# Transposing gathered tokens by products of 64 array rows each, into two PSUM banks

## The chip, the core and the metric

One Trainium2 chip, one core of it. The metric is the time of one execution on the device, in microseconds (us), as the median of several runs. TensorE, VectorE, ScalarE and GpSimd run instruction streams of their own, which meet at semaphores; SyncE issues DMA transfers.

## What is computed

A block attention and behind it a layer of experts in which each token goes to one expert of sixteen. All is FP32.

```python
# q, k, v: 8 x 8 x 576 x 64; softmax within chunks of 64 tokens
attn = softmax(scale * q_c @ k_c.T);  x = (attn @ v_c) as 4608 x 512
g = argmax(x @ w_group)                    # one of 4 groups
e = argmax(x[g] @ w_expert[g])             # one of 4 experts in it
h = maximum(x @ w1[g, e], 0)               # 512 -> 1024
out = g_weight * e_weight * (h @ w2[g, e])  # 1024 -> 512
```

## The kernel before

The attention stage writes the tokens into a scratch array in DRAM, sorted by expert. Then a loop (line 926 on TensorE, and one like it on each other engine) runs over *units*. A unit is up to 256 tokens of one expert: two token tiles of 128 rows, or one, or the half of one. The kind of a unit, which a table holds, chooses the branch: `pairs` for two tiles, `one` for one tile, `few` for at most 64 tokens.

Matrix products are made in the FP32R type, each value as a high part and a low rest, so layer 1 is three sums (high by high, high by low, low by high). For layer 1 the tokens must have features on the partitions. The unit's rows are gathered from DRAM into `xgr` (128 tokens x 2 tiles x 514), and TensorE transposes them: `XT(u, kind)`, line 757, makes four products per tile, each with a 128x128 piece of `xgr` as the weights and the identity as the moving operand, into one PSUM bank per tile (`pxt[0]`, `pxt[1]`, line 704). In the branches for two tiles `XT(u + 1)` stands between layer 1 (`L1p`, line 849) and layer 2 (`L2`, line 866) of unit u; in `one` it stands between the two groups of transposes `T` of the hidden layer (line 773), in `few` between two of `Tq` (line 779). It transposes one tile or two, by the kind of the unit to come, and waits for the gathers on the semaphores Ga and Gb.

ScalarE copies the transposed tokens as the high part into `xth` (`xe`, line 998, by `XE`, line 974), and VectorE subtracts to get the low part `xtl` (line 1074). Each waits with XE: ScalarE on XT, VectorE on ScalarE's copies, for each tile on its own. After XE stands, on both, the preparation of the next weights (`prep1`, `prep2`: casts on ScalarE, subtractions on VectorE). GpSimd waits on XT before it saves two columns of `xgr` (`carry2`) and issues the next gathers. Layer 1 of unit u + 1 waits for ScalarE's copies, and its third sum for VectorE's.

The attention stage makes its products in tiles of 64x64 of the array (lines 301 and 337), with transposes of 128x128 in FP32 between them (lines 325 and 367). Line 587 transposes the first tokens in FP32R, before the loop.

Of the kernel before, what the change touches and what calls it, by code (L numbers as in the profile page):

```python
# [9 lines left out]
F32 = mybir.dt.float32  # L10
# [9 lines left out]
P = 128  # L20
# [93 lines left out]
def moe_kernel(tc, qk, v, wgs, w1, w2, cst, out):  # L114
# [3 lines left out]
    with ExitStack() as ctx:  # L118
# [584 lines left out]
        word = fpool.tile([1, 1], F32, name="word")  # L703
        pxt = [ps.tile([P, 4, P], F32, name="pxt%d" % j) for j in range(2)]
        ph = [lgk if j == NL0 - 1 else ps.tile([P, 512], F32, name="ph%d" % j) for j in range(4)]
# [28 lines left out]
        with tc.tile_critical():  # L734
            with nc.Block() as blk:

                @blk.tensor
                def _(pe):
                    def W(n, x):
                        pe.wait_ge(S[n], x)  # L740
# [16 lines left out]
                    def XT(u, kind):  # L757
                        def tr(j, inc):
                            for c in range(4):
                                m = pe.transpose(pxt[j][:, c, :].bitcast(F32R), xgr[:, j, c * P:(c + 1) * P], identr)  # L760
                            m.then_inc(S["XT"], inc)

                        with pe.If(kind > 1):
                            W("Ga", 16 * u)
                            tr(0, 1)
                            W("Gb", 16 * u)
                            tr(1, 1)
                        with pe.Else():
                            W("Ga", 16 * u)
                            W("Gb", 16 * u)  # L770
                            tr(0, 2)

# [201 lines left out]
                def XE(eng, W, sem, op, u, kn, oph=None):  # L974
                    with eng.If(kn > 1):
                        W("XT" if sem == "XEa" else "XEa", 2 * u + 1)
                        op(0).then_inc(S[sem], 1)
                        W("XT" if sem == "XEa" else "XEa", 2 * u + 2)
                        op(1).then_inc(S[sem], 1)
# [14 lines left out]
                def _(ac):  # L994
# [3 lines left out]
                    def xe(u, kn):  # L998
                        XE(ac, W, "XEa", lambda j: ac.copy(xth()[:, :, half[j]], pxt[j]), u, kn)

# [69 lines left out]
                def _(ve):  # L1070
                    def W(n, x):
                        ve.wait_ge(S[n], x)

                    def xe(u, kn):
                        XE(ve, W, "XEd", lambda j: ve.tensor_sub(xtl()[:, :, half[j]], pxt[j], xth()[:, :, half[j]].bitcast(F32)), u, kn,
                           lambda: ve.tensor_sub(xth()[:, :, 64:P], pxt[0][:, :, 0:64], xth()[:, :, 0:64].bitcast(F32)))
# [352 lines left out]
```

## Time and profile before

| | us |
|---|---|
| median of 3 runs | 625.95 (625.27 to 626.41) |
| the profiled execution, by its own time | 621.86 |
| its span, first to last instruction | 620.2 |
| TensorE products busy | 581.9 (94%) |
| TensorE weight loads busy | 503.1 (81%) |
| VectorE busy | 365.8 (59%) |
| ScalarE busy | 263.5 (42%) |
| GpSimd busy | 154.2 (25%) |

The page gives times in microseconds. PE is TensorE's products, PEld its weight loads, which overlap products; DVE is VectorE, ACT ScalarE, POOL GpSimd, SP SyncE. Starts of products are exact, their ends are modelled, and a product's stated duration holds the time through the array, so products that follow each other overlap in these rows. The expert loop runs from about 180 us to the end.

### The profile page before, as it was taken

What the parts mean: (1) busy time and instruction counts of PE and PEld (TensorE: products, weight loads), DVE (VectorE), ACT (ScalarE), POOL (GpSimd) and SP (SyncE); (2) the same over time, 40 slices, a digit from 0 to 9 for tenths busy, and PEclk for the clock granted to TensorE, in tenths of its full rate; (3) what the DMA queues carried; (4) which work ended last, traced back from release to release, by engine and by line L of the source; (5) the groups of instructions that cost most, each with busy time, mean ns of one, the idle gap of its engine ahead of it and who ended that gap; (6) DMA issues with size and microseconds to landing.
All of it is one profiled execution on the core that took longest, in us unless ns stands there. A gap on an engine that the chain in (4) does not pass through costs nothing.

```text
span 620.2 us, 16208 instructions
## 1 busy us (share of the span) xinstructions
PE 581.9 (94%) x5711; PEld 503.1 (81%) x5712; DVE 365.8 (59%) x688; ACT 263.5 (42%) x367; POOL 154.2 (25%) x279
## 2 busy tenths in 40 slices
PE   7898988968699999989999999999999999999995
PEld 4676766846688989878889899989989988898984
DVE  4677878886568472127597674725425578853311
ACT  3454555646236251115485362625115365552111
POOL 0003334574413111111333212222111121321120
PEclk9898999889899999989999999999999999999998
DMA  8999878464559792116298854552712686821110
GB/s 311 423 396 380 271 277 299 139 234 155 170 155 376 256 323 95 66 29 241 106 339 308 317 201 155 187 193 79 268 51 95 235 315 249 320 91 66 34 38 30
DMA packets 43103, 128.23 MB, mean 207 GB/s; under 512 B 4590, under 2 KB 4974, under 8 KB 41136
## 3 DMA queue, kind: packets, MB, share of 16 engines
q1 hardware_dynamic: 32192, 93.93, 42.7%
q0 software_dynamic: 10864, 33.64, 15.1%
q8 instruction: 33, 0.54, 0.3%
q14 instruction: 14, 0.11, 0.1%
HBM read 106.40 MB, written 21.93 MB: 207 GB/s over the span
## 4 chain that ended last, share of the span: by engine, by line
PE 85%; issue 5%; DVE 4%; DMA 3%; ACT 1%; POOL 1%; SPq 1%; DVEq 0%; ACTq 0%; POOLq 0%
PE py L875 29%; PE ph L860 20%; PE lgk L860 7%; PE ph L844 5%; PE o L337 3%; PE sc L301 3%; PE py L892 2%; PE pxt L760 2%; PE lgk L367 2%; PE tp L325 1%; DMA qk<-in_qk_dram 1%; PE lgk L325 1%; PE tp L367 1%; PE sc L387 1%; PE ph L806 1%
## 5 line engine op out<-in xcount | busy, mean ns | idle before, releaser
L860 PE MATMUL ph<-xt,w1h 128*128 128x256 f32 x672 | 100.3, 286 | 2.7 <-issue 2.7
L860 PEld LDWEIGHTS ph<-xt,w1h 128*128 128x128 f32 x672 | 90.7, 194 | 4.4 <-issue 3.3
L1016 ACT ACTIVATE hth<-ph 128x512 fp32r<-128x512 f32 x43 | 25.7, 598 | 157.4 <-PE ph L860 154.1
L1343 POOL DMA_INDIRECT out_dram<-xl,io__2835 x37 | 39.2, 1059 | 163.2 <-DVE xl L1079 147.1
L1089 DVE TENSOR_TENSOR w1l<-w1r,w1h 128x2048 fp32r<-128x2048 f32 x28 | 63.0, 2289 | 13.1 <-ACT w1h L1003 11.1
L1093 DVE TENSOR_TENSOR w2l<-w2r,w2h 128x1024 fp32r<-128x1024 f32 x60 | 69.4, 1219 | 2.2 <-ACT w2h L1007 2.2
L875 PE MATMUL py<-w2h,hth 128*128 128x512 f32 x264 | 67.6, 398 | 0.0
L875 PE MATMUL py<-w2l,hth 128*128 128x512 f32 x264 | 65.3, 389 | 0.0
L875 PE MATMUL py<-w2h,htl 128*128 128x512 f32 x264 | 65.2, 389 | 0.0
L1079 DVE TENSOR_SCALAR xl<-py,io__2835 128x512 f32<-128x512 f32 x33 | 24.7, 749 | 67.8 <-PE py L875 67.8
L1112 DVE SCALAR_TENSOR_TENSOR htl<-ph,hth 128x512 fp32r<-128x512 f32 x40 | 27.4, 688 | 61.2 <-ACT hth L1016 60.8
L875 PEld LDWEIGHTS py<-w2l,hth 128*128 128x128 f32 x264 | 49.6, 188 | 10.5
L875 PEld LDWEIGHTS py<-w2h,htl 128*128 128x128 f32 x264 | 49.6, 188 | 10.3
L875 PEld LDWEIGHTS py<-w2h,hth 128*128 128x128 f32 x264 | 47.6, 188 | 10.1 <-ACT hth L1064 0.9
L860 PE MATMUL ph<-xt,w1l 128*128 128x256 f32 x336 | 54.7, 285 | 0.5 <-DVE w1l L1089 0.5
L1003 ACT CAST w1h<-w1r 128x2048 fp32r<-128x2048 f32 x28 | 52.1, 1903 | 2.6 <-issue 1.9
L1007 ACT CAST w2h<-w2r 128x2048 fp32r<-128x2048 f32 x28 | 52.3, 1923 | 0.0
L860 PEld LDWEIGHTS ph<-xt,w1l 128*128 128x128 f32 x336 | 46.8, 193 | 0.7 <-DVE w1l L1089 0.7
L337 PEld LDWEIGHTS o<-va,pT 64*64 64x64 f32 x1120 | 22.5, 147 | 19.4 <-issue 7.3
L337 PE MATMUL o<-va,pT 64*64 64x65 f32 x1120 | 28.3, 239 | 10.1 <-DVE x L355 5.4
L301 PE MATMUL sc<-qk 64*64 64x64 f32 x1152 | 27.6, 233 | 7.4 <-issue 4.4
L301 PEld LDWEIGHTS sc<-qk 64*64 64x64 f32 x1152 | 22.0, 141 | 14.9 <-issue 6.0
(286 smaller groups left out, 949.4 us busy)
## 6 DMA issues: line engine op xcount, KB each, us to landing
w1r<-in_moe_w_dram SPq DMA_DIRECT2D x30, 1024.0 KB, 5.2
w2r<-in_moe_w_dram SPq DMA_DIRECT2D x30, 1024.0 KB, 7.1
qk<-in_qk_dram SPq DMA_DIRECT2D x15, 1024.0 KB, 10.3
xgr<-xs POOLq DMA_DIRECT2D x38, 257.0 KB, 4.6
va<-in_v_dram SPq DMA_DIRECT2D x24, 390.0 KB, 7.5
qk<-in_qk_dram SPq DMA_DIRECT2D x6, 512.0 KB, 6.9
w1r<-in_moe_w_dram POOLq DMA_DIRECT2D x2, 1024.0 KB, 9.7
w2r<-in_moe_w_dram POOLq DMA_DIRECT2D x2, 1024.0 KB, 7.6
```

The lines of the kernel that those rows point to most:

```text
L301: nc.tensor.matmul(sc[cols, x, hp * CH:hp * CH + CH], lhsT=T[rows, 0, hp, cols], rhs=T[rows, 1, hp, cols], start=True, stop=True)
L337: nc.tensor.matmul(o[cols, x, hp * W:hp * W + W], lhsT=pT[rows, hp, cols], rhs=v_at(2 * t + c)[rows, hp], start=True, stop=True)
L844: m = pe.matmul(ph[n], a_[:, c, 0:P], w_[:, c, n * 512:(n + 1) * 512], start=(i == 0), stop=(i == 11))
L860: m = pe.matmul(ph[f // 2][:, f % 2 * 256:f % 2 * 256 + 256], w_[:, c, f * P:(f + 1) * P], a_[:, c, :], start=(i == 0), stop=(i == 11))
L875: m = pe.matmul(py[j], a_[:, f, half[j]], w_(b, f), start=(i == 0), stop=(i == 23))
L1003: lambda b, s, j: ac.copy(wt[b][0][:, s], w1r[j]), K1)
L1007: lambda b, s, j: ac.copy(wt[b][2 + j], w2r[j]), K2)
L1016: ac.activation(hth()[:, 2 * b:2 * b + 2, :], ph[b].rearrange("p (f t) -> p f t", f=2), AF.Relu).then_inc(S["Ha"], 1)
L1089: lambda b, s, j: ve.tensor_sub(wt[b][1][:, s], w1r[j], wt[b][0][:, s].bitcast(F32)), K1, js)
L1093: m = ve.tensor_sub(wt[b][4 + 2 * j + i], w2r[j][:, 2 * i:2 * i + 2], wt[b][2 + j][:, 2 * i:2 * i + 2].bitcast(F32))
L1112: ve.scalar_tensor_tensor(out=htl()[:, 2 * b:2 * b + 2, :], in0=ph[b].rearrange("p (f t) -> p f t", f=2), scalar=0.0, in1=hth()[:, 2 * b:2 ...
L1343: gp.indirect_dma_start(out, bass.IndirectOffsetOnAxis(ap=io[:, j, 0:1].bitcast(I32), axis=0), yb[:, j, :], None, bounds_check=N - 1, oob_ ...
```

## The change

Each transpose of a 128x128 piece becomes two, one of rows 0 to 63 and one of rows 64 to 127 of the token tile, on the array's rows of the same numbers. The two write to different banks: `pxt2` holds two banks, the first for the low rows of both token tiles, the second for the high rows. TensorE waits for both gathers first, and signals once, after the last product. ScalarE's and VectorE's accesses collect the two halves of a tile from the two banks, and each engine waits once, for all of what comes before it.

```diff
-        pxt = [ps.tile([P, 4, P], F32, name="pxt%d" % j) for j in range(2)]
+        pxt2 = ps.tile([P, 2, 4, P], F32, name="pxt")
+        pxt = [pxt2[:, j] for j in range(2)]
+        xhalf = lambda j: pxt2[:, :, :, 64 * j:64 * j + 64]
+        xrows = lambda z, j: z[:, :, half[j]].rearrange("p c (r t) -> p r c t", r=2)
...
                     def XT(u, kind):
-                        def tr(j, inc):
-                            for c in range(4):
-                                m = pe.transpose(pxt[j][:, c, :].bitcast(F32R), xgr[:, j, c * P:(c + 1) * P], identr)
-                            m.then_inc(S["XT"], inc)
-
+                        def tr(js):
+                            for j in js:
+                                for c in range(4):
+                                    for r in (slice(0, 64), slice(64, P)):
+                                        m = pe.transpose(pxt2[:, r.start // 64, c, 64 * j:64 * j + 64].bitcast(F32R),
+                                                         xgr[r, j, c * P:(c + 1) * P], identr[r, r])
+                            m.then_inc(S["XT"], 2)
+
+                        W("Ga", 16 * u)
+                        W("Gb", 16 * u)
                         with pe.If(kind > 1):
-                            W("Ga", 16 * u)
-                            tr(0, 1)
-                            W("Gb", 16 * u)
-                            tr(1, 1)
+                            tr((0, 1))
                         with pe.Else():
-                            W("Ga", 16 * u)
-                            W("Gb", 16 * u)
-                            tr(0, 2)
+                            tr((0,))
...
                 def XE(eng, W, sem, op, u, kn, oph=None):
                     with eng.If(kn > 1):
-                        W("XT" if sem == "XEa" else "XEa", 2 * u + 1)
+                        W("XT" if sem == "XEa" else "XEa", 2 * u + 2)
                         op(0).then_inc(S[sem], 1)
-                        W("XT" if sem == "XEa" else "XEa", 2 * u + 2)
                         op(1).then_inc(S[sem], 1)
...
-                        XE(ac, W, "XEa", lambda j: ac.copy(xth()[:, :, half[j]], pxt[j]), u, kn)
+                        XE(ac, W, "XEa", lambda j: ac.copy(xrows(xth(), j), xhalf(j)), u, kn)
...
-                        XE(ve, W, "XEd", lambda j: ve.tensor_sub(xtl()[:, :, half[j]], pxt[j], xth()[:, :, half[j]].bitcast(F32)), u, kn,
+                        XE(ve, W, "XEd", lambda j: ve.tensor_sub(xrows(xtl(), j), xhalf(j), xrows(xth(), j).bitcast(F32)), u, kn,
```

## Rows read from the trace of the kernel before

**Rows 1.** The page's first line: the profiled span.
```profile
span 620.2 us, 16208 instructions
```
**Rows 2.** The page's chain that ended last, by line.
```profile
PE py L875 29%; PE ph L860 20%; PE lgk L860 7%; PE ph L844 5%; PE o L337 3%; PE sc L301 3%; PE py L892 2%; PE pxt L760 2%; PE lgk L367 2%; PE tp L325 1%; DMA qk<-in_qk_dram 1%; PE lgk L325 1%; PE tp L367 1%; PE sc L387 1%; PE ph L806 1%
```
**Rows 3.** TensorE's waits, 180 to 620 us: total us, times, longest.
```profile
PE ph L860 <- issue: 2.7, 2, 1.8
PE ph L860 <- DVE w1l L1089: 0.5, 1, 0.5
...
```
**Rows 4.** Instructions of line 760: duration ns min/median/max, first and last start us.
```profile
L760 PEld LDWEIGHTS pxt<-identr,xgr x152: 138/140/145, 182.9 to 607.2; 128*128 128x128 f32 x152
L760 PE MATMUL pxt<-identr,xgr x152: 221/249/308, 183.1 to 607.2; 128*128 128x128 f32 x152
```
**Rows 5.** Timeline around eight transposes: start us, us, engine, line, what, count.
```profile
221.35 0.28 PE L860 MATMUL ph<-xt,w1h 128*128 128x256 f32 x1
...
221.47 0.80 PE L760 MATMUL pxt<-identr,xgr 128*128 128x128 f32 x8
221.67 0.60 ACT L1016 ACTIVATE hth<-ph 128x512 fp32r<-128x512 f32 x1 [1.07 <-PE ph L860]
...
222.10 0.71 PE L875 MATMUL py<-w2h,hth 128*128 128x512 f32 x2
```
**Rows 6.** Timeline around four transposes between the layers, 244.4 to 245.3 us.
```profile
244.16 0.65 PE L860 MATMUL ph<-xt,w1h 128*128 128x256 f32 x4
...
244.94 0.69 PE L875 MATMUL py<-w2h,hth 128*128 128x512 f32 x2
```
**Rows 7.** Timeline, TensorE, in a unit of one tile, around eight transposes.
```profile
261.70 0.27 PE L776 MATMUL lgk<-cs,xl 128*128 128x128 f32 x1
...
262.45 0.62 PE L776 MATMUL ph<-cs,xl 128*128 128x128 f32 x4
```
**Rows 8.** Timeline, TensorE, in a unit of one tile, around four transposes.
```profile
309.07 0.60 PE L776 MATMUL lgk<-cs,xl 128*128 128x128 f32 x4
...
309.98 0.66 PE L776 MATMUL ph<-cs,xl 128*128 128x128 f32 x4
```
**Rows 9.** Timeline, attention stage: from products of 128x128 to products of 64x64.
```profile
62.42 0.49 PE L367 MATMUL lgk<-cs,x 128*128 128x128 f32 x3
62.84 0.29 PE L301 MATMUL sc<-qk 64*64 64x64 f32 x4
```
**Rows 10.** Timeline, attention stage: 64x64 products and loads, and the 128x128 behind them.
```profile
49.24 0.22 PE L337 MATMUL o<-va,pT 64*64 64x65 f32 x2
...
48.76 0.56 PEld L337 LDWEIGHTS o<-va,pT 64*64 64x64 f32 x32
...
49.39 0.20 PEld L367 LDWEIGHTS tp<-cs,x 128*128 128x128 f32 x2
```
**Rows 11.** Timeline, 149.5 to 150.2 us: the first tokens' transposes, and a one-row product behind them.
```profile
149.55 0.40 PEld L587 LDWEIGHTS sc<-identr,xg0r 128*128 128x128 f32 x4 [0.97 <-ACT xT L368]
...
150.01 0.29 PEld L485 LDWEIGHTS sc<-cs,one 1*128 1x128 f32 x2
```
**Rows 12.** Timeline, TensorE: the first two layer-2 products behind products of 17 rows.
```profile
179.30 0.73 PE L892 MATMUL py<-w2l,hth 128*128 128x512 f32 x2
```
**Rows 13.** Timeline, 505 to 522 us: copies, first subtraction, and TensorE's wait.
```profile
516.38 1.06 ACT L999 CAST xt<-pxt 128x512 fp32r<-128x512 f32 x2
...
516.98 1.29 DVE L1075 TENSOR_TENSOR xt<-pxt,xt 128x512 fp32r<-128x512 f32 x2
...
520.52 0.50 PE L860 MATMUL ph<-xt,w1l 128*128 128x256 f32 x2 [0.54 <-DVE w1l L1089]
```
**Rows 14.** The whole chain in order of time (start, us, what); and the stretch 270:275 by engine, clock.
```profile
268.63 1.76 issue
270.39 7.50 PE ph L860 x48
...
270.00:275.00 5.00, 4.61 (x26) 4.62 (x27) 0.00 (x0) 0.00 (x0) 1.89 (x4) 0.66 0.09 30
```

## Prediction

> **What bounds the kernel now.** The first view is the head of the page and its chain of work: the profiled span is 620.2 us [rows 1], and TensorE carries most of it: the products of the expert layers lead, and the transposes of line 760, which the change rewrites, hold 2% of the chain [rows 2]. The second view is the list of what TensorE waited for from 180 us on, the expert loop: three kinds in 440 us, of 2.7, 0.5 and less [rows 3]. No gather of tokens and no copy out of PSUM is among them (waits too short for that list appear below), so the loop runs at TensorE's own pace: what its queue takes longer or shorter reaches the end one for one, except where something else is later. The third view is the instructions of line 760: 152 products, median 249 ns, and as many loads of 140 ns [rows 4]. Walking the loop's timeline finds them in 24 places: 14 with eight products (two token tiles), 10 with four.
>
> The fourth view is the timeline around one such place. After the last product of layer 1 at 221.35 come the eight transposes, first start 221.47, and the second layer at 222.10 [rows 5]. From the start of the last layer-1 product to the end of the second layer-2 product is 222.81 - 221.35 = 1.46 us. The eight starts spread over 0.80 - 0.25 = 0.55 us. So all transposes together hold some 12 us, and that is the stake: 2%.
>
> **What paces a transpose.** The same form of transpose runs after an idle stretch at line 587: its four weight loads take 0.40 us, so they start (0.40 - 0.14) / 3 = 0.086 us apart from the very first, while the load itself lasts 0.14 [rows 11]. In FP32, with the same 128 columns of weights, the second load starts 0.20 - 0.14 = 0.06 after the first [rows 10]. In every transpose the data are the weights (128 columns) and the identity moves. The change halves the rows and the moving columns, and leaves the 128 columns of each load; it makes two loads of one.
>
> **The change, part by part.** (1) Eight products become eight pairs, one of each pair on array rows 0 to 63, one on rows 64 to 127. That different tiles of the array load and multiply side by side the attention stage shows: 32 loads of 64x64 take 0.56 us, that is 8 rounds of four at about 0.06 [rows 10]. So I let the two of a pair overlap and ask for the round. No row shows a transposed load of 64 rows. Bounds: 0.06 a round, if only the load's stream counts and the rest of the 0.086 goes with the shorter product; 0.172, if the two loads of a pair follow each other at today's distance. I take 0.086, the row with the same operation, type and number of loaded columns. Then the body gains nothing: 7 x 0.086 = 0.60 against 0.55.
>
> The Trainium skill speaks for a gain here: its page TensorEngine Tiling, section Theoretical Speedup, gives up to 2x for a contraction of 64 rows or fewer. By it a round would be about 0.04 and the sum below 6.0 us lower. No row of this trace shows transposes of half height, so it stands among the rivals.
>
> (2) The array changes its tiling twice in each of the 24 places. The rows: from a 128x128 product to 64x64 ones the start moves from 62.42 + 0.49 - 0.27 = 62.64 to 62.84, 0.20 [rows 9]; a following product of the same tiling would start at the pace of layer 1, (0.65 - 0.28) / 3 = 0.12 [rows 6]. From 64x64 back to 128x128 it is 49.24 to 49.39, 0.15, and the first load is then no longer ahead of its product [rows 10]. A change of rows alone, with all 128 columns kept, pays too: line 485 loads one row after line 587, at 150.01, when the last transpose's load started at 149.55 + 0.40 - 0.14 = 149.81: 0.20 where the pace is 0.086 [rows 11]. The first layer-2 pair after a change of tiling takes 0.73 [rows 12] against 0.71 now [rows 5].
>
> The new walk for a place of eight between layers 1 and 2: 0.20 into the new tiling, 7 x 0.086 = 0.60, 0.06 until the last load has a product, 0.01 for its partner, 0.15 back, 0.73: 1.75 us against 1.46, so +0.29. Eight places are of this kind: 2.3 us. With four products the walk is 1.75 - 4 x 0.086 = 1.41; today it is from 244.16 + 0.65 - 0.28 = 244.53 to 245.63, 1.10 [rows 6]: +0.31 by these, +0.30 with the rounding, in seven places: 2.1 us.
>
> (3) In the units of one token tile the transposes stand between two groups of transposes of the hidden layer. Today from 261.70 to 262.45 + 0.62 = 263.07, 1.37 [rows 7]. New: 0.20 + 0.60 + 0.07 + 0.15 + 0.66 (four of them from a standing start [rows 8]) = 1.68: +0.31, six places: 1.9 us. With four products in such a unit today's stretch holds a wait: 309.07 + 0.60 - 0.27 = 309.40 to 310.64, 1.24 [rows 8], since the copy that the second group needs isn't done. New 1.68 - 0.34 = 1.34: +0.10, three places: 0.3 us. The first three parts are 2.3 + 2.1 + 1.9 + 0.3 = 6.6 us.
>
> (4) ScalarE's two copies now wait for the whole of XT, and VectorE's first subtraction for both copies. Between the layers this costs nothing: ScalarE is in the Relu from 221.67 to 222.27 [rows 5], past the last transpose's start (221.47 + 0.80 - 0.25 = 222.02), and layer 1 of the next unit, which needs the copies, comes after all of layer 2. One place has no such cover. At the end of the unit at 509 to 519 the copies run from 516.38 to 517.44 and the first subtraction starts at 516.98, between them; then VectorE makes w1l, for which TensorE waits 0.54 at 520.52 [rows 13]. Subtractions that start at 517.5 put all of that 0.5 later. Queued behind them on VectorE are w1l and w2l, and TensorE waits for the first; behind ScalarE's copies stand its casts of w2, which layer 2 needs much later. +0.5 us. Elsewhere the extra wait lies under layer 2.
>
> (5) Both gathers are now awaited ahead of all products. The list of TensorE's waits holds none for a gather [rows 3]; I cost this at nothing, hidden by the layer-2 and layer-1 work between their issue and their use. The strided access of the copies (two banks read at once) I cost at nothing too: both engines have the room, up to the place in (4). The gathers of the next unit follow the transposes on GpSimd's queue; these start 0.3 later, as does all that needs them.
>
> (6) XT stands seven times in TensorE's program, each with 12 more products and 12 more loads; see the third rival.
>
> **Sum.** 6.6 + 0.5 = 7.1 us. Against the profiled execution (621.86 us, of which the span is 620.2) that is 629.0; that execution lies 0.65% under the median of the runs shown, 625.95, to which I add it: **633.0 us**, 1.1% slower. What a measurement here can tell from no change is about 0.2%, 1.25 us.
>
> **Rivals.**
> First, the rounds are shorter. At 0.06 (0.059 unrounded) the sum loses 7 x 0.027 x 14 + 3 x 0.027 x 10 = 3.5: +3.6, 629.6 us. For it: the FP32 loads come at that distance [rows 10]. Against: the 0.086 was there when no earlier product was streaming [rows 11]. At half of today's body (0.55 / 14 = 0.04 a round) it loses 6.0: +1.1, 627.0; that asks for loads closer together than any row has them. This is the case that the rule of TensorEngine Tiling would give.
>
> Second, and on the other side: half the rows with all columns are no change of tiling, so nothing drains, and rounds are 0.06. Then the walk keeps its ends and the body goes from 0.55 to 0.41 in 14 places and from about 0.21 (244.94 - 244.53 [rows 6], less 0.12 ahead and 0.08 behind as in [rows 5]) to 0.18 in 10: -1.96 - 0.3 + 0.5 = -1.8, 624.2 us. It decides as soon as the drain costs less per place than the 0.14 that the body saves; today's rows say 0.2 to 0.3. Against it: line 485 after line 587 [rows 11].
>
> Third, fetching of code. At 268.63 TensorE stood for 1.76 us on "issue", that is, on nothing that another engine does, and the next 48 products took 7.50 [rows 14] where 48 x 0.12 = 5.76 is normal; the mean granted clock from 270 to 275 was 0.66, so part of that stretch ran at 1.2 GHz in place of 2.4, after the idle stretch. Together 3.5 us hang on where that code lies. More code ahead of it can move the stall away (629.5) or make a second one (636.5).
>
> Fourth, the loads of a pair don't overlap: rounds of 2 x 0.059 = 0.118 add 4.1 (637.2), of 0.172 add 11.0 (644).
>
> **How the numbers follow.** Forecast as summed 0.48; rounds of 0.06 0.15; halved rounds 0.06; no drain 0.06; stall gone 0.04, second stall 0.04; loads in turn at 0.118 0.12, at 0.172 0.05. The range runs from 626.5 to 638.0: it leaves out the no-drain case, the slowest, and a remainder of the halved one, about 0.15. Faster by over 0.2%: no drain and a little of the stall gone together with short rounds, 0.08. Within 0.2%: the halved rounds and such mixtures, 0.10. Slower: 0.82.
>
> **What will show it.** In the timeline of a place of eight: about 0.20 from the last layer-1 product to the first load of a transpose, loads in pairs with about 0.086 between pairs, and a visible gap of some 0.15 ahead of layer 2. The walk from the last layer-1 product to the end of the second layer-2 product should be 1.75; if it is under 1.46 the forecast is wrong in sign. At the unit like that of 509 to 519, VectorE's first subtraction should start after the second copy. The forecast is wrong if the gaps are missing, if pairs come faster than 0.07 or slower than 0.1, or if the total moves by more than the places add up to: then stalls on "issue" have moved.

## The result, and the profile after

The changed kernel takes 630.94 us (median of 20 runs, 621.86 to 635.67), the kernel before on the same chip 624.52 (20 runs, 618.76 to 630.49): 6.4 us or 1.0% more by these medians. The ratio on record, which is taken from fast runs alone since some executions of either kernel are slower as a whole, is 1.0133, 95% interval 1.009 to 1.0176: about 1.3% slower. The profiled execution of the changed kernel took 625.41 us by its own time. The head of its page, to hold against [rows 1]:

```profile
span 623.8 us, 16500 instructions
## 1 busy us (share of the span) xinstructions
PE 582.7 (93%) x5863; PEld 501.0 (80%) x5864; DVE 363.3 (58%) x688; ACT 264.0 (42%) x367; POOL 152.8 (24%) x279
```

TensorE issues 152 products more than before and is busy 0.8 us longer. The loss doesn't show in busy time; it must be in gaps. The two spans differ by 3.6 us only, since in this execution the attention stage, which the change doesn't touch, ended earlier: the first transposes start at 178.4 us, before at 183.1 [rows 4]. (In the profiles of this study that start lies between 178.4 and 192.9.) The fair measure is from the last product ahead of the first transposes to the end of TensorE's last product, "the loop" from here on: 430.85 us before, 439.24 after, +8.39. That is one execution of each kernel; the runs say 6.4 by the medians and 1.33% of 624.52 = 8.3 by the ratio.

The instructions of the rewritten line, against [rows 4]: duration in ns (min/median/max), first and last start.

```profile
L765 PEld LDWEIGHTS pxt<-identr,xgr x304: 133/136/139, 178.4 to 610.9; 64*128 64x128 f32 x152
L765 PE MATMUL pxt<-identr,xgr x304: 240/247/253, 178.4 to 610.9; 64*128 64x64 f32 x152
```

Half the rows in a load, and the load lasts as long as before: 136 ns against 140. A place of eight between the layers, the timeline to hold against [rows 5]:

```profile
215.73 0.64 PE L863 MATMUL ph<-xt,w1h 128*128 128x256 f32 x4
216.30 0.84 PE L765 MATMUL pxt<-identr,xgr 64*128 64x64 f32 x16
216.41 0.60 ACT L1018 ACTIVATE hth<-ph 128x512 fp32r<-128x512 f32 x1 [1.07 <-PE ph L863]
217.07 0.97 PE L878 MATMUL py<-w2h,hth 128*128 128x512 f32 x3
217.19 1.07 ACT L1001 CAST xt<-pxt 128x512 fp32r<-128x512 f32 x2 [0.17 <-PE pxt L765]
```

The last layer-1 product starts at 215.73 + 0.64 - 0.28 = 216.09. From there it takes 0.21 to the first transpose (before 0.12), the 16 starts spread over 0.84 - 0.25 = 0.59 (before 0.55), and from the last of them to layer 2 it is 217.07 - 216.89 = 0.18 (before 0.09). So the body is as long as it was, and both ends have a gap that wasn't there. Single records show the pairs: 0 to 17 ns from the first of a pair to the second, 84 ns (median) from pair to pair. The walk to the start of the second layer-2 product is 1.06 us before and 1.32 after; to that product's end, as the prediction has it, 1.46 before and 1.71 after, where 1.75 was forecast.

What TensorE waited for in the loop, against [rows 3]:

```profile
PE ph L863 <- issue: 3.9, 2, 2.5
PE ph L863 <- DVE w1l L1091: 1.1, 1, 1.1
PE pxt L765 <- DMA xgr<-xs: 0.9, 1, 0.9
PE lgk L787 <- DVE xl L1227: 0.3, 1, 0.3
```

Three rows differ: "issue" 3.9 in place of 2.7, w1l 1.1 in place of 0.5, and a gather that wasn't in the list at all. The gather's place in the timeline:

```profile
338.17 0.64 PE L863 MATMUL ph<-xt,w1h 128*128 128x256 f32 x4
...
339.72 0.85 PE L765 MATMUL pxt<-identr,xgr 64*128 64x64 f32 x16 [0.90 <-DMA xgr<-xs]
```

And in the chain, by time (start, us, what):

```profile
331.57 7.88 DMA xgr<-xs
339.45 0.26 issue
```

The last layer-1 product starts at 338.53, the second gather's last packet lands at 339.45: the start of the transposes is 1.18 behind that product in place of 0.21, 0.97 lost. The chain's 0.26 behind the landing is the way from it to the first product. The gather was not issued later than before: 6.96 us ahead of that layer-1 product, 6.97 before; it took longer to land. The unit that the prediction's step (4) speaks of:

```profile
518.25 1.05 ACT L1001 CAST xt<-pxt 128x512 fp32r<-128x512 f32 x2
519.34 1.29 DVE L1077 TENSOR_TENSOR xt<-pxt,xt 128x512 fp32r<-128x512 f32 x2 [0.47 <-ACT xt L1001]
522.88 0.51 PE L863 MATMUL ph<-xt,w1l 128*128 128x256 f32 x2 [1.12 <-DVE w1l L1091]
```

VectorE's first subtraction now starts behind both copies (518.25 + 1.05 = 519.30), and TensorE waits 1.12 for w1l where it waited 0.54 [rows 13].

Last the stalls on "issue": 2.54 at 230.80 and 1.35 at 269.76, before 0.96 and 1.76 [rows 3, 14]. The first of them in the timeline, and the stretch behind it (stretch, its length, busy us of PE, PEld, DVE, ACT, POOL, then the granted clock):

```profile
230.80 0.73 PE L863 MATMUL ph<-xt,w1h 128*128 128x256 f32 x4 [2.54 <-issue]
```

```profile
232.10:235.50 3.40, 3.40 (x19) 3.40 (x18) 0.00 (x0) 0.20 (x1) 0.31 (x2) 0.50 0.06 25
```

As at [rows 14], the granted clock fell behind a stall: to 0.50, 1.2 GHz, in the stretch shown, after some 1.3 us of products. The loss to the low clock is the same in both (the 96 products behind the stall start over 12.98 us in either kernel, over 11.39 at full clock: 1.6), so the net is 3.89 - 2.72 = 1.2 us.

The ledger of the loop, by walking all 24 places in both traces:

| | forecast, us | measured, us |
|---|---|---|
| 24 places, without the gather | 6.6 | 5.5 |
| gather at 339 us | 0 | 0.97 |
| w1l | 0.5 | 0.58 |
| stalls on "issue" and the clock behind them | 0 | 1.2 |
| rest | | 0.1 |
| sum | 7.1 | 8.4 |

### The profile page after: what moved, and what is told of

It reads as the page before. It is cut to its first block, busy times and chain, and to the rows that moved or that the text cites. A ratio compares the mean times of both kernels' runs of the same rounds, so it can differ in the third digit from the quotient of the medians.

```text
span 623.8 us, 16500 instructions
## 1 busy us (share of the span) xinstructions
PE 582.7 (93%) x5863; PEld 501.0 (80%) x5864; DVE 363.3 (58%) x688; ACT 264.0 (42%) x367; POOL 152.8 (24%) x279
## 4 chain that ended last, share of the span: by engine, by line
PE 78%; DVE 6%; issue 6%; DMA 5%; POOL 2%; ACT 1%; DVEq 0%; SPq 0%; POOLq 0%; ACTq 0%
PE py L878 28%; PE ph L863 18%; PE lgk L863 6%; PE ph L847 4%; PE o L337 3%; PE sc L301 3%; PE pxt L765 2%; PE py L895 2%; PE lgk L367 1%; DMA xgr<-xs 1%; PE ph L809 1%; DMA qk<-in_qk_dram 1%; PE tp L325 1%; PE py L832 1%; DMA xs<-x,pos 1%
## 5 line engine op out<-in xcount | busy, mean ns | idle before, releaser
L863 PE MATMUL lgk<-xt,w1h 128*128 128x256 f32 x224 | 33.7, 283 | 0.0
```

The costliest lines, as they stand in the source:

```text
L863: m = pe.matmul(ph[f // 2][:, f % 2 * 256:f % 2 * 256 + 256], w_[:, c, f * P:(f + 1) * P], a_[:, c, :], start=(i == 0), stop=(i == 11))
```

## The experiments

My theory: the pace of a transpose is that of loading 128 columns, which half the rows don't shorten; the two row tiles load side by side, so a pair takes what one full transpose took; and each change of tiling costs about 0.1 us at either end. The rivals: the pace is that of the queue or of the 64-column products, and the gaps at the ends are the waits that the change moves.

Each run below stands beside runs of the kernel before on the same chip; their median is in brackets. A time without a ratio is that of a single run, so there the trace is the evidence and not the time.

### What sets the pace: the order of the halves

```diff
-                            for j in js:
-                                for c in range(4):
-                                    for r in (slice(0, 64), slice(64, P)):
+                            for r in (slice(0, 64), slice(64, P)):
+                                for j in js:
+                                    for c in range(4):
```

> The changed kernel, with all low-row halves of XT first and then all high-row halves, so that neighbours in the queue lie on the same array rows. Theory (two row tiles load side by side, each tile takes a load every 0.085 us): the 16 starts of a place spread over 15 x 0.085 = 1.28 us in place of 0.595, the 8 starts of a smaller one over 0.60 in place of 0.257; 14 x 0.68 + 10 x 0.34 = 13 us more than the changed kernel. Rival (the 0.085 is the time of a pair, that is 0.04 a product, whatever the rows): spreads unchanged, no difference to the changed kernel.

640.86 us (628.28), ratio 1.0189, 1.0142 to 1.0236.

```profile
207.61 1.19 PE L765 MATMUL pxt<-identr,xgr 64*128 64x64 f32 x16
```

The starts spread over 1.19 - 0.25 = 0.94 in a place of eight and over 0.27 in a place of four. The theory wanted 1.28 (0.60 in a place of four), the rival 0.595: neither holds as stated. Single records show how it comes about: four starts alone, 83 to 86 ns apart, then four pairs (8 to 14 ns inside a pair, about 84 from pair to pair), then four alone again at 83 to 87. Each row tile takes a load each 0.085 us, as the theory says, and the two work side by side. But the halves of a pair needn't be neighbours in the queue: the second tile's loads begin when about four of the first tile's eight are still to start. The rows don't name the half, so which product is which is inferred from the counts and the order in the code. In a place of four, where the distance is only four, nearly all overlap. The theory's pace stands, its picture of the queue doesn't.

### What sets the pace: the kind of load

The changed kernel with ordinary products in place of transposes; and the kernel before with two ordinary full-height products per block, each with 64 moving columns.

```diff
-                                        m = pe.transpose(pxt2[:, r.start // 64, c, 64 * j:64 * j + 64].bitcast(F32R),
-                                                         xgr[r, j, c * P:(c + 1) * P], identr[r, r])
+                                        m = pe.matmul(pxt2[:, r.start // 64, c, 64 * j:64 * j + 64],
+                                                      xgr[r, j, c * P:(c + 1) * P], identr[r, r], start=True, stop=True)
```

> The changed kernel, with each half transposed by an ordinary FP32R product with the identity in place of the transpose operation; precision of the tokens is not kept. Rows, columns, banks and order are the same; the weight load is the ordinary one, which lasts 0.19 us at 128 columns against 0.14. Theory (the load sets the pace of a pair): pairs 0.11 us apart, spread of a place of eight blocks 7 x 0.112 + 0.01 = 0.80 us against 0.595, of four 0.35 against 0.257. Rival (the moving product sets it): 0.085 or less, spread 0.6. The ends of a place (0.21 ahead, 0.18 behind) stay by both.

```diff
-                                m = pe.transpose(pxt[j][:, c, :].bitcast(F32R), xgr[:, j, c * P:(c + 1) * P], identr)
+                                for r in (slice(0, 64), slice(64, P)):
+                                    m = pe.matmul(pxt[j][:, c, r], xgr[:, j, c * P:(c + 1) * P], identr[:, r], start=True, stop=True)
```

> The kernel before, with each 128x128 transpose made as two ordinary FP32R products of full height, with half of the identity's columns moving each; precision of the tokens is not kept. No change of tiling. Theory (the load of 128 columns sets the pace, the moving columns don't): 16 products 0.112 us apart, spread 15 x 0.112 = 1.68 us for eight blocks, 0.78 for four; lead 0.12 and end 0.09 as in the kernel before, no gap. Rival (halving the moving columns shortens the pace): 0.06 or less a product, spread 0.9 or less.

639.66 and 647.67 us (628.28 for both). The loads (duration in ns, min/median/max), of the halves and of the full height:

```profile
L765 PEld LDWEIGHTS pxt<-identr,xgr x304: 182/188/188, 189.7 to 625.0; 64*128 64x128 f32 x152
```

```profile
L761 PEld LDWEIGHTS pxt<-identr,xgr x304: 186/192/193, 187.7 to 633.2; 128*128 128x128 f32 x152
```

A place of eight in each, with the last layer-1 products ahead and layer 2 behind, first the halves, then the full height:

```profile
203.78 0.64 PE L863 MATMUL ph<-xt,w1h 128*128 128x256 f32 x4
204.34 1.08 PE L765 MATMUL pxt<-identr,xgr 64*128 64x64 f32 x16
205.35 1.19 PE L878 MATMUL py<-w2h,hth 128*128 128x512 f32 x4
```

```profile
202.63 0.64 PE L861 MATMUL ph<-xt,w1h 128*128 128x256 f32 x4
203.11 1.87 PE L761 MATMUL pxt<-identr,xgr 128*128 128x64 f32 x16
204.82 0.47 PE L876 MATMUL py<-w2h,hth 128*128 128x512 f32 x1
```

An ordinary load lasts 188 to 192 ns, a transposed one 136 to 140, with half the rows or all of them. The pairs of halves come 0.112 apart, but for a first interval of 0.13 (spread of eight 0.81, of four 0.36), and the full-height products 0.112 apart, but for a first one of 0.03 (1.59 and 0.70; 1.68 and 0.78 were expected). The product is the same 64 columns as in the changed kernel, where the pace is 0.085, and the data moved are the same: what changed is the operation, and with it the load's time, and the pace went with that. In the second of these kernels there is no gap at the ends (0.12 and 0.11), where the array keeps one tiling; in the first there is one at both (0.21 and 0.20; 0.21 and 0.18 were expected).

### What sets the pace: FP32, in halves and in full height

In FP32 the loads of a transpose come as close as 0.06 [rows 10]. First the changed kernel in FP32, then the kernel before.

```diff
-                                        m = pe.transpose(pxt2[:, r.start // 64, c, 64 * j:64 * j + 64].bitcast(F32R),
-                                                         xgr[r, j, c * P:(c + 1) * P], identr[r, r])
+                                        m = pe.transpose(pxt2[:, r.start // 64, c, 64 * j:64 * j + 64],
+                                                         xg[r, j, c * P:(c + 1) * P], ident[r, r])
```

> The changed kernel, with the halves transposed in FP32 in place of FP32R: same rows, columns, banks and waits. In the kernel before an FP32 transpose's second load started 0.06 us after the first, an FP32R one's 0.086 after. Theory (the load paces a pair, and its price goes by the type): pairs 0.06 apart, the spread of a place of eight 0.43 in place of 0.595, of four 0.19 in place of 0.257; the two changes of tiling stay, so a place of eight still takes 0.1 us more than before the change. 14 x 0.165 + 10 x 0.07 = 3.0 us under the changed kernel, 2.5 over the kernel before (5.5 less 3.0). Rival (FP32 streams its moving columns at half the rate, 0.109 for 128, and that paces it): 0.085 or more a pair.

```diff
-                                m = pe.transpose(pxt[j][:, c, :].bitcast(F32R), xgr[:, j, c * P:(c + 1) * P], identr)
+                                m = pe.transpose(pxt[j][:, c, :], xg[:, j, c * P:(c + 1) * P], ident)
```

> The kernel before with its transposes in FP32 in place of FP32R, in full height, so with no change of tiling: the partner of e7_fp32_halves, which had the halves in FP32. Theory (a transpose takes the longer of its load and its product; in FP32 the load takes up to 0.06 us and the product of 128 moving columns takes longer than that, as the hidden layer's FP32 transposes, which start 0.109 apart at 261.4 us in the kernel before, suggest): the starts of eight spread over 7 x 0.109 = 0.76 in place of 0.55, of four over 0.33 in place of 0.21; 14 x 0.21 + 10 x 0.12 = 4.1 us above the kernel before, 0.65%. Against the halves' 0.488 and 0.238 that would mean that half-height products do help, where the product and not the load sets the pace. Rival (the load sets the pace here too, at 0.06): spread 0.42 and 0.18, the ends as in the kernel before, 14 x 0.13 + 10 x 0.03 = 2.1 us below it, 0.35%.

637.11 us (628.8) for the halves; 631.01 (625.68) for the full height, ratio 1.007, 1.0034 to 1.0106. A place of eight in the timeline of each:

```profile
205.38 0.71 PE L765 MATMUL pxt<-cs,xgr 64*128 64x64 f32 x16
```

```profile
204.33 1.04 PE L760 MATMUL pxt<-cs,xgr 128*128 128x128 f32 x8
```

In halves the pairs come 0.060 to 0.065 apart, but for the first interval of 0.11, and the starts spread over 0.488 (of four over 0.238), where the theory wanted 0.43 and 0.19; in full height each transpose takes 0.109, and the spread is 0.763 (0.327), the theory's 0.76 and 0.33. So in full height the product sets the pace, and here the halves do what one would hope of them: 0.488 in place of 0.763. (Whether load or product sets the 0.06 of the halves, no run tells.) With both changes of tiling the walk of eight is 1.19 in halves and 1.23 in full height, a gain of 0.04; that of four 0.94 against 0.79, a loss. In FP32R, where the load sets the pace, there is nothing to gain and the two changes are still paid. That is the whole case. Against the kernel before, FP32 loses either way: its walks are 1.06 and 0.72. The loop of the halves in FP32 is 7.3 us longer than that of the kernel before, where 2.5 was expected: 3.3 in the places, 0.5 for a gather, 0.5 for w1l, and the rest stalls on "issue" and the low clock.

The Trainium skill, TensorEngine Tiling (Array Packing), section Theoretical Speedup, whose "up to 2x" the prediction held as a rival, is thus borne out in part, and only where the load isn't the limit: 0.763 / 0.488 = 1.6 for FP32, 0.55 / 0.59 = 0.9 for FP32R. The Trainium skill, TensorE: Matmul & The Clock Gate, section LDWEIGHTS (loading the stationary operand), says that a load's time goes with its columns and not with its rows; the 136 and 140 ns agree for the rows. No run here varied the columns of these loads; in the kernel before, ordinary loads of one row and 128 columns (line 485) last 184 ns, and loads of 17 rows and one column (line 915) 78.

### The price of a change of tiling

Half the blocks by half-height transposes, half by two full-height products; first all of one kind and then all of the other, then in turn. The copies and waits are those of the changed kernel. The two kernels differ in one line:

```diff
-                            for j, c in sorted(((j, c) for j in js for c in range(4)), key=lambda z: (z[1] % 2, z)):
+                            for j, c in sorted(((j, c) for j in js for c in range(4)), key=lambda z: z):
```

> The changed kernel, with half of the 128x128 blocks (odd c) made by two ordinary full-height products of 64 moving columns, all of them behind the halved transposes of the even blocks; precision of these tokens is not kept. Two changes of tiling in a place, as in the changed kernel, but one of them now inside the place. By the pieces measured so far (pairs 0.085, full-height products 0.112, 0.21 ahead, 0.18 at the change back, 0.112 behind) the walk from the last layer-1 product to the second layer-2 product's start is 1.9 us for eight blocks and 1.3 for four. It is the base for the next kernel.

> The same products as in the grouped kernel, with the blocks in turn: eight changes of tiling in a place of eight, four in one of four. Theory (each change drains the array and leaves the next load uncovered, 0.12 us over the normal pace): 6 x 0.12 = 0.7 us more than the grouped kernel in a place of eight, 0.23 in a place of four, 12 us in all. Rival (a change costs only against the long products of the layers, inside XT the short ones hide it): walks as in the grouped kernel, within 0.1 us.

648.4 us grouped, 658.66 in turn (628.8 for both). The start of a place of eight, in turn:

```profile
205.26 0.25 PE L768 MATMUL pxt<-identr,xgr 64*128 64x64 f32 x2
205.44 0.41 PE L766 MATMUL pxt<-identr,xgr 128*128 128x64 f32 x2
205.78 0.25 PE L768 MATMUL pxt<-identr,xgr 64*128 64x64 f32 x2
205.95 0.41 PE L766 MATMUL pxt<-identr,xgr 128*128 128x64 f32 x2
```

The same products, the same loads, six changes more: the walk is 1.88 grouped and 2.505 in turn, 0.63 / 6 = 0.105 per change; in a place of four 1.26 and 1.474, 0.21 / 2 = 0.105. The theory expected 0.7 and 0.23. A start behind a change comes 0.175 to 0.18 late into the full height (205.26 to 205.44) and 0.207 into the halves (from 205.44 + 0.41 - 0.28 = 205.57 to 205.78), each time about 0.1 more than the pace. Both kernels change the operation with the tiling, transposes for the halves and ordinary products for the full height. That the operation isn't what costs, the two runs with ordinary products alone show: 0.21 and 0.20 at the ends with halves, 0.12 and 0.11 in full height. So the gaps of the changed kernel, 0.21 and 0.18, are the price of its two changes of tiling and of no wait.

### The waits without the halves

The kernel before with the change's waits: both gathers first, one signal, ScalarE behind all of XT, VectorE behind both copies.

```diff
+                        W("Ga", 16 * u)
+                        W("Gb", 16 * u)
                         with pe.If(kind > 1):
-                            W("Ga", 16 * u)
-                            tr(0, 1)
-                            W("Gb", 16 * u)
-                            tr(1, 1)
+                            tr((0, 1))
...
-                        W("XT" if sem == "XEa" else "XEa", 2 * u + 1)
-                        op(0).then_inc(S[sem], 1)
                         W("XT" if sem == "XEa" else "XEa", 2 * u + 2)
+                        op(0).then_inc(S[sem], 1)
```

> The kernel before, with the waits of the change alone: both gathers first, one signal after all transposes, ScalarE's copies and VectorE's subtractions each after all of what comes before. Theory: spreads and ends of the 24 places as before (0.55, 0.21), TensorE's wait for w1l in the unit of 64 tokens near 511 to 521 us grows from 0.54 to about 1.1 us, nothing else moves; +0.5 us in all, too little to see in the time. Rival (the wait hides there as it does elsewhere): 0.54.

628.12 us (628.28). All places are those of the kernel before (spread 0.55 and 0.21, ends 0.12 and 0.08), but for two of TensorE's waits:

```profile
PE py L890 <- ACT hth L1013: 1.3, 1, 1.3
PE ph L858 <- DVE w1l L1086: 1.0, 1, 1.0
```

w1l costs 1.0 where it cost 0.54, so the prediction's step (4) comes from the waits alone. The other row lies ahead of the loop and is found in kernels with and without these waits (1.2 in the kernel with more code, below). At the tenth place, the one at 339 us of the changed kernel, the first transpose starts 0.26 behind the last layer-1 product in place of 0.12, and the spread is 0.63 in place of 0.55, 0.22 in all: TensorE waited for the second gather, which landed with the last layer-1 product (345.38 both). In the kernel before it landed 0.16 ahead of that product (339.83, the product at 339.99). From landing to first transpose it takes 0.26, so the cover that step (5) counted on was, by an estimate from these numbers, 0.02 us thick for transposes that start 0.12 behind the product, and 0.11 for those of the changed kernel, which start 0.21 behind it.

### The second gather, awaited late

The changed kernel, with the second gather awaited only ahead of the second tile.

```diff
-                            m.then_inc(S["XT"], 2)
+                            return m
 
                         W("Ga", 16 * u)
+                        with pe.If(kind > 1):
+                            tr((0,))
                         W("Gb", 16 * u)
                         with pe.If(kind > 1):
-                            tr((0, 1))
+                            tr((1,)).then_inc(S["XT"], 2)
                         with pe.Else():
-                            tr((0,))
+                            tr((0,)).then_inc(S["XT"], 2)
```

> The changed kernel, with the second gather awaited only ahead of the second token tile's transposes, as in the kernel before; the first tile's eight half transposes run as soon as the first gather is there. Theory (the wait of 0.97 us near 339 us comes from the second gather's late landing): the first tile's transposes, about 0.35 us with their change of tiling, move into the wait, which shrinks by about 0.35 us or vanishes where the gather lands earlier; every other place stays as in the changed kernel, 0.25 us above the kernel before, but for a few hundredths that the second branch may take; time within 0.2% of the changed kernel, 1.2% above the kernel before. Rival (the first gather, or something else, is what comes late): the first tile's transposes start no earlier than they did, and the wait stays whole.

632.51 us (627.03), ratio 1.0094, 1.0056 to 1.0132. TensorE's waits hold no gather:

```profile
PE ph L865 <- issue: 3.5, 2, 2.1
PE py L897 <- ACT hth L1020: 1.2, 1, 1.2
PE ph L865 <- DVE w1l L1093: 1.1, 1, 1.1
PE lgk L789 <- DVE xl L1229: 0.3, 1, 0.3
```

This tells nothing of the order of the waits: in this execution the second gather landed at 345.69, 0.6 ahead of the last layer-1 product (346.29), so there was nothing to shorten. The time from issue to landing of that transfer varies: 6.81 us before, 6.38 here, 5.72 to 6.82 in four further kernels in full height, 7.24 to 7.88 in the changed kernel and four others with its halves, 6.60 in one more of these. In the kernel before, the changed one and this one it is issued 3.9 us behind the first of the two loads of the next layer-2 weights, and the DMA engines are busy to over 9 tenths for most of its way. Why it is slower in most executions with halves stays open. The 24 places, with no gather among them, add 5.5 us to those of the kernel before, the same as in the changed kernel. The loop is 5.4 longer, but that is a balance: w1l adds 0.6 and the stalls on "issue" 0.8 (2.12 and 1.43), and no stall was followed by the low clock, which cost the kernel before 1.6. The runs say 0.94% of 627.03 = 5.9.

### More code, never run

The kernel before with twelve more transposes per XT in TensorE's program, behind a branch that is never taken.

```diff
+                        if not isinstance(u, int):
+                            with pe.If(u > 60):
+                                for i in range(12):
+                                    pe.transpose(pxt[0][:, i % 4, :].bitcast(F32R), xgr[:, 0, 0:P], identr)
```

> The kernel before, with twelve transposes in a branch that is never taken ahead of those of each of the six XT in the loop: as much more code in the loop as the change adds. Theory (TensorE's stalls on issue in the first passes are fetches of code, and lie where the code lies): spreads and ends of the 24 places as before, but the stalls of 0.96 us near 190 and 1.76 near 268 lie elsewhere or have another size, and five or so more fetches stand in the instruction queue (33 before, 38 after). Rival (the stalls belong to the branch to a unit of another kind, not to the amount of code): both at the same units, the same sizes within 0.3 us.

625.7 us (628.8).

```profile
PE ph L864 <- issue: 1.7, 1, 1.7
PE py L896 <- ACT hth L1020: 1.2, 1, 1.2
PE py L879 <- ACT hth L1020: 0.7, 1, 0.7
```

One of the two stalls on "issue" is gone, though nothing that runs was changed but the branch; the other, 1.73 at 275.73, stands where it stood and has its size. The third row is a wait of layer 2 for ScalarE in the unit that lost its stall, so little was won there. So each side was right about one stall: the theory about the first, the rival about the second. The expected number of fetches was missed: the queue that carries instructions moved 35 packets, where I expected the changed kernel's 38 (33 before).

All thirteen traces together say more. The second stall stands in each of them ahead of layer 1 of the fifth unit of the loop, with 1.32 to 1.76 us. The first is another matter: in all eight kernels whose XT makes twice the products (the changed one, the row order, the ordinary products, the full height, both of mixed tilings, FP32 in halves, the late gather) it stands ahead of layer 1 of the third unit, with 1.95 to 2.97 us, and the instruction queue moves 38 packets; in the five others nothing stands there. Two of the eight, the ordinary products in full height (total, times, longest) and the late gather (a timeline row):

```profile
PE ph L861 <- issue: 3.7, 2, 2.0
```

```profile
239.93 0.73 PE L865 MATMUL ph<-xt,w1h 128*128 128x256 f32 x4 [2.12 <-issue]
```

The full height has no halves, so the stall goes with the number of products in XT and not with their rows. In the five others the first stall is in layer 1 of the first unit (0.96 before, 1.90 with the waits alone, 0.31 in FP32 at full height, 5.69 in the next run) or missing (here). Code of the same amount that is never run doesn't bring the stall to the third unit. That the stalls are fetches of code fits these counts, but no row names it, and there is one trace of each kernel.

### Transposes under layer 2

If a transpose costs its load, the load could lie under a longer product. The kernel before, with each transpose behind one of the first eight (or four) products of layer 2, in units of two tiles:

```diff
                                 m = pe.matmul(py[j], a_[:, f, half[j]], w_(b, f), start=(i == 0), stop=(i == 23))
+                                if i < 4 * tiles:
+                                    z, c = divmod(i, 4)
...
+                                    x = pe.transpose(pxt[z][:, c, :].bitcast(F32R), xgr[:, z, c * P:(c + 1) * P], identr)
...
-                            XT(u + 1, kn)
-                            L2(u, b, r, 0)
+                            with pe.If(kn > 1):
+                                L2(u, b, r, 0, 2)
+                            with pe.Else():
+                                L2(u, b, r, 0, 1)
```

> The kernel before, with one move: in the units of two token tiles the transposes of the next unit no longer stand between the layers but one behind each of the first eight (or four) products of layer 2, so that the loads of a transpose, about 0.086 us apart when they follow each other, run beside products of 512 columns that take about 0.23 us. Theory (a transpose costs the time of its load, not of its product): each transpose then costs only its short product of about 0.06 us, so a place of eight loses 0.55 + 0.12 and gains 8 x 0.06, about 0.2 less, a place of four about 0.1 less: 14 places, 2 us in all, 0.3% below the kernel before. Rival (every change between the two kinds of product costs something of its own, or the load of the next layer-2 product can no longer run ahead): each transpose costs 0.09 or more and the time is that of the kernel before or above it. Second rival (the copies of the transposed tokens and the next gathers come some 1.6 us later): a wait of TensorE for a gather or for the copies shows, at the place near 339 us first.

636.55 us (627.03), ratio 1.0136, 1.0084 to 1.0187: the forecast had the wrong sign.

```profile
200.32 1.23 PE L860 MATMUL ph<-xt,w1h 128*128 128x256 f32 x5 [5.69 <-issue]
...
212.56 0.22 PE L882 MATMUL pxt<-identr,xgr 128*128 128x128 f32 x1
212.62 0.45 PE L875 MATMUL py<-w2h,hth 128*128 128x512 f32 x1
212.90 0.22 PE L882 MATMUL pxt<-identr,xgr 128*128 128x128 f32 x1
```

From transpose to transpose it is 0.34 us where a layer-2 product alone takes 0.23: each transpose costs 0.11, more than the 0.086 that it costs in a row. The transpose's own load is hidden, but the load of the layer-2 product behind it isn't: it begins when the transpose starts (212.56 both), an ordinary load takes 0.112 of the pace (the full-height run above), and the 0.06 of the transpose covers half of that. That last step is inferred from the two numbers; no run took it apart. The rival's second half fits. The 14 places lose 2.6 us in all (0.24 each for eight, 0.13 for four, to the last of the first 24 products of layer 2). The loop is 7.5 us longer; the rest of it is stalls: 7.1 us on "issue" against 2.7, and the low clock behind the first (0.50 until 204.5), which cost some 0.5 more than that of the kernel before. The stall of 5.69 us is the largest of the study. Layer 2 now stands twice in the program; that this is what brought the stall is likely and not shown. The second rival, a gather or a copy that comes late, shows nowhere.

No version tried is faster than the kernel before by more than the spread of its runs.

## Why the prediction was right, and where not

The forecast was 7.1 us more than the kernel before, 1.1%; the medians differ by 6.4, the ratio gives 8.3 with an interval of 5.6 to 11. The 633.0 itself is 2.1 above the median measured; 1.4 of that is the baseline, 625.95 in three runs and 624.52 in twenty.

(1) The rounds: forecast 0.086, measured 0.084. Right, and for the reason given, as far as it was tested: the pace is that of the load. The run with ordinary loads shows it go with the load (0.112) while rows and product columns stay. The number of columns, which the prediction named, was the same in all these loads.

(2), (3) The changes of tiling: forecast +0.29 for eight and +0.30 for four between the layers, measured +0.25 to +0.26 and +0.26 to +0.27; in one-tile units with eight +0.31, where five of six gave +0.25 to +0.26 and one +0.13; in those with four +0.10, where +0.05 to +0.12 came out. The mechanism was right, and the two runs with tilings grouped and in turn price it by itself at 0.105 per change. The term that was mis-sized is the way back: I put 0.06 for a last load that runs ahead of its product and 0.15 behind it, 0.21; 0.18 was measured in all, some 0.8 us over the 24 places. Of the rest 0.2 is the one place of +0.13. Over 24 places: 5.5 in place of 6.6.

(4) w1l: forecast +0.5, measured +0.58, and shown by the run with the waits alone.

(5) The gathers, costed at nothing: wrong at one place, by 0.97 us in the profiled execution. The step read "hidden" from a list of waits in which no gather stood. A wait that isn't there says nothing of how near it is: the landing was 0.16 us ahead of the last layer-1 product, and that number could have been read from the trace before. How much of the 0.97 is the change's own doing, I can't say: awaiting the second gather first cost 0.22 in the run with the waits alone, and the rest came with a later landing. The step's other half, strided copies at no cost, was right: the two copies take 1.05 us against 1.06 [rows 13].

(6) and the third rival, code: put at nothing in the sum. The stalls grew by 1.2 us, with the same loss to the clock. I gave 0.08 to such moves, of 3.5 us either way; the measured one is smaller than that, and it was no accident of one execution: a first stall of 1.95 to 2.97 us ahead of the third unit stands in every kernel with the doubled XT and in no other, where the kernel before has one of 0.96 elsewhere. So it belongs in the sum, though the trace before couldn't tell its size. The prediction's last sign pointed at it: if the total moves by more than the places add up to, stalls on "issue" have moved. The loop moved by 8.4, the places by 5.5.

So the mechanism of the places was right, and the total came out well partly by luck: 1.1 us too much in the places stood against 2.2 us, the gather and the stalls, that were not in the sum. The other rivals fell: no row has rounds of 0.04 or 0.06 in FP32R (first), the cost of a change of tiling is there at both ends (second), and the loads of a pair do overlap (fourth).

## What to carry to other kernels

In these runs splitting a product into row tiles of the array shortened the body only where the product set the pace; read first whether loads or products follow each other at their closest, and halve the one that does. Each change of tiling cost about 0.1 us here, beside long products and between short ones alike, so a short burst of tiled products between full ones starts 0.2 us behind. And for each wait that is called hidden, read the margin from the trace, not only its absence from the list. Last, a change that adds instructions to a loop can bring a stall of its own while the loop is first run through; a second kernel with as many instructions and without the idea, as the full-height products were here, tells the two apart.

## What the runs showed of the hardware

- A transposed FP32R load of 128 columns comes each 0.085 us and an ordinary load of the same data each 0.11, with 64 rows or 128. Transposed FP32 loads come as close as 0.06.
- FP32 transposes with 128 moving columns follow each other at 0.109, with 64 rows and 64 moving columns the pairs at 0.06.
- A change between 128-row and 64-row tiles of the array costs about 0.1 us over the pace, in either direction, with transposes or ordinary products.
- Two row tiles work side by side even when their products stand some four places apart in the queue (0.94 for eight and eight in place of 1.28), and starts then seem to leave the order of the program; this is inferred from counts, as the rows don't name the half.
- A transpose between layer-2 products cost 0.11 us, not its own 0.06; that this is the load of the long product behind it is inferred.
- TensorE stood on "issue" for 1.3 to 1.8 us ahead of the fifth unit of the loop in all thirteen kernels, and for 2.0 to 3.0 us ahead of the third in the eight whose XT makes twice the products. Behind several stalls the granted clock fell to 0.50 (2.54 us in the changed kernel, 1.76 before), behind others not (2.47 with ordinary products, 2.12 with the late gather).
